# Attention and gated MLP on one core: other blocks for five weight-conversion steps and for the q and k transposes of the next pair

## The chip, the cores and the metric

The kernel runs on one core of a Trainium2 chip. The metric is the device time of one execution in microseconds (us): 690.47, the median of three runs (690.37 to 690.92). Engine names are those of the profile: PE is TensorE (matmuls), PEld its weight loads, DVE is VectorE, ACT is ScalarE, POOL is GpSimd and SP is SyncE, whose queue issues most DMAs.

## The reference

q, k and v have the shape (4 batches, 8 heads, 576 positions, 64). The result of the attention is the input of a gated MLP with three weights.

```python
def rotate(x):
    x1, x2 = (x[..., :half], x[..., half:])
    return np.concatenate([x1 * cos - x2 * sin, x1 * sin + x2 * cos], axis=-1)
scores = 1/np.sqrt(D) * np.matmul(rotate(q), rotate(k).transpose(0, 1, 3, 2))
attn = np.exp(scores - np.max(scores, axis=-1, keepdims=True))
attn = attn / (np.sum(attn, axis=-1, keepdims=True) + 1e-09)
x = np.matmul(attn, v)          # then (batch, position) rows of 8 heads x 64 = 512
g = x @ w_gate                  # 512 x 1536
y = (g / (1 + np.exp(-g))) * (x @ w_val) @ w_out
```

## The kernel before, in words

All matrix work is done in a pair of 32-bit pieces: a value is split into a high part, which a copy to the matmul type makes, and a low part, which a subtraction makes. A product is the sum of high x high, high x low and low x high. So each transpose or product that goes on into another product leaves PSUM twice: ACT casts the high part (for the probabilities L426, for q and k L308, for tails L440), then DVE subtracts it from the source (L427, L312, L441). Only after the subtraction is the PSUM buffer free.

**The attention stage** works on 16 pairs of heads, 9 blocks each: blocks 0 to 7 are 128 rows of one head (head 0 and 1 in turn), block 8 holds the 64 last rows of both. For each of the 144 blocks, numbered n = 9 p + b, TensorE computes scores (L349) into one of two score buffers, DVE takes the row maximum (L364), ACT takes the exponential (L382), TensorE transposes the probabilities in four parts (L425), and ACT and DVE make high and low parts of them. The scores of a block can start only when the exponential of two blocks before has read its buffer. Transposes of any kind share three PSUM buffers. The parts of a row beyond 512 are transposed as tails (L435, L437). When the first four or the last five blocks of a pair are transposed, the products with v follow in 10 matmuls per head (L465) into one buffer, which ACT copies out (L470) and a DMA stores.

**q and k of the next pair** are prepared in this stage. GpSimd rotates them (L206 to L208). In three steps (`qk_T`, L281) TensorE transposes the rotated tile: the tails in 2 transposes (L293), q in 4 and k in 4 (L289); ACT casts each result (L308) and DVE makes the low part (L312). The last of the three steps also issues eight DMAs on SP (`qk_stack`, L314) that copy the finished parts within SBUF into the operands of the scores: QK, QZ and BD.

**The first two weights** are unpacked in the same stage (`wfirst`, L765, with `bits10`, L717): each takes ten steps on ACT (L752, L724, L727), GpSimd (L725, L729 to L731) and DVE (L754 to L756). For every four pairs a row of reciprocals is made (L392, L393), transposed (L400), copied (L402) and stored.

**What sets the order.** A table `PLAN` names, for each step, the block in which the program writes it down. `qk` has three rows, for pair 0, pair 1 and all later pairs: the blocks of the first, second and third step; `qkw` names what each step is (2 is the tails, 0 is q, 1 is k). `cv` has a row for each of the two weights: the block of the load, then the blocks of the ten steps. The loop at L1053 goes through the blocks and through the step functions in the order of L31:

```python
    w, bs = P["qkw"][min(p, 2)], P["qk"][min(p, 2)]
    for i in range(3):
        if bs[i] == b:
            at.qk_T(p + 1, w[i], i == 2)
...
    for i, ns in enumerate(P["cv"]):
        if n == ns[0]:
            cvq[i] = moe.wfirst(0, i)
        for _ in range(ns[1:].count(n)):
            tc.keep_in_program_order(cvq[i].pop(0)())
```

GpSimd keeps the written order throughout; PE keeps it in pair 0 and SP up to block 48. Everything else is put in order by a scheduler at build time, which starts from the written order; so a step that is written elsewhere also moves other instructions. After attention the MLP stages follow, bound to a written order on PE and SP.

Of the kernel before, what the change touches and what calls it, by code (L numbers as in the profile page):

```python
# [28 lines left out]
    trb=3,  # L29
    warm=[9, 0, 1, 2, 0, 1],  # L30
    order=["qk", "scores", "trans", "pv", "exp", "evac", "rstore", "rope", "tails", "conv", "x", "conv1", "vsplit"],  # L31
    qk=[[3, 4, 6], [1, 2, 3], [0, 0, 1]],
    qkw=[[0, 2, 1], [2, 0, 1], [2, 0, 1]],
    tails=[4, 0],
    pv=[1, 6, 5, 3, 7, 8, 2, 7, 3],
# [3 lines left out]
    rope=1,  # L39
    vsplit=8,  # L40
    rstore=0,
    cv=[[13, 21, 25, 26, 28, 30, 34, 34, 44, 44, 45], [20, 30, 35, 36, 39, 41, 43, 43, 54, 54, 63]],
    xs=[[3, 3], [3, 6], [6, 5], [7, 5], [8, 7], [9, 5], [10, 5], [11, 5], [12, 7], [13, 7], [14, 1], [14, 2],
        [14, 8], [15, 0], [15, 2], [15, 4]],
    xe=[[5, 3], [6, 3], [7, 3], [8, 3], [9, 3], [10, 3], [11, 3], [12, 3], [13, 5], [14, 1], [14, 3], [14, 5],
# [1461 lines left out]
```

## Time and profile before

| | |
|---|---|
| time, median of 3 runs | 690.47 us (690.37 to 690.92) |
| the profiled execution | 690.11 us, its span 688.3 us |
| TensorE busy | 677.4 us, 98% of the span |
| VectorE, ScalarE, GpSimd busy | 582.4, 424.2 and 470.1 us |
| attention: scores of block 0 of pair 1 / pair 6 / pair 15 start at | 25.85 / 110.57 / 259.08 us |
| granted TensorE clock | 1.00 throughout |

Times in a timeline are from the start of the span. The busy time of TensorE is modelled: a matmul that overlaps the one before it is shown longer than the engine needs for it, so what an instruction costs is read from the start of one to the start of the next. "<-" behind an instruction names what ended the engine's idle time before it. A merged line such as "x4" stands for neighbours of one kind, at the start of the first.

### The profile page before, as it was taken

Reading aid. Unit: us, or ns where it says so; the run is one execution under the profiler, and the core shown is the slowest. Engines: PE = TensorE matmul, PEld = TensorE weight load, DVE = VectorE, ACT = ScalarE, POOL = GpSimd, SP = SyncE. Lnnn points to the kernel's source line nnn. Section 1 sums busy time; section 2 is a strip of 40 time slices with the busy share of each in tenths; the row PEclk is TensorE's granted clock in tenths of the full one; section 3 lists DMA queues with packets and bytes.
Section 4 is the critical chain, followed back from the end, with each engine's and each line's share of the span. In section 5 each row is a group of like instructions: output and inputs, shape, how many; then the busy total and the mean of one; then the engine's idle time right before and its main releaser. Section 6 shows DMA issues by size and latency. Waiting matters only on the chain. (4 is left out here: it accounts for less than half of the span.)

```text
span 688.3 us, 12675 instructions
## 1 busy us (share of the span) xinstructions
PE 677.4 (98%) x4414; PEld 664.3 (97%) x4414; DVE 582.4 (85%) x883; ACT 424.2 (62%) x873; POOL 470.1 (68%) x475
## 2 busy tenths in 40 slices
PE   7999999999999999999999999999999999999998
PEld 6899999999999999999999999999999999999997
DVE  5888898888888888979988898988999599877683
ACT  5899988888888888555543434424435375344341
POOL 8899799999999985998889588677784720000000
PEclk9999999999999999999999999999999999999999
DMA  6897999889988879791214345354464797627101
GB/s 195 185 248 205 218 225 243 208 206 243 246 206 208 220 189 285 187 235 70 90 58 164 122 141 204 130 187 150 161 212 163 264 317 252 207 74 247 47 24 69
DMA packets 78784, 125.76 MB, mean 183 GB/s; under 512 B 16880, under 2 KB 55680, under 8 KB 78720
## 3 DMA queue, kind: packets, MB, share of 16 engines
q1 hardware_dynamic: 75248, 118.77, 60.6%
q10 hardware_dynamic: 3472, 6.18, 2.4%
q8 instruction: 35, 0.57, 0.4%
q14 instruction: 29, 0.24, 0.1%
HBM read 66.91 MB, written 33.10 MB: 145 GB/s over the span
## 5 line engine op out<-in xcount | busy, mean ns | idle before, releaser
L364 DVE TENSOR_REDUCE nmt<-sc 128x1 f32<-128x576 f32 x144 | 108.2, 751 | 20.3 <-PE sc L349 18.9
L382 ACT ACTIVATE E<-sc,nmt 128x576 f32<-128x576 f32 x128 | 97.5, 761 | 1.7 <-DVE nmt L364 1.6
L425 PE MATMUL tr<-ident,E 128*128 128x128 f32 x512 | 77.1, 274 | 0.4 <-DVE ET1l L427 0.2
L425 PEld LDWEIGHTS tr<-ident,E 128*128 128x128 f32 x512 | 61.2, 141 | 3.4 <-PE tr L289 1.3
L1472 PE MATMUL ch<-dW,dO 128*128 128x384 f32 x216 | 63.8, 337 | 0.2 <-DVE dW L1420 0.2
L206 POOL TENSOR_TENSOR t<-X,tab 128x256 f32<-128x256 f32 (+2 forms) x94 | 54.4, 600 | 9.4 <-DMA X<-in_qk_dram 5.8
L349 PE MATMUL sc<-QK 128*128 128x288 f32 x240 | 58.7, 325 | 1.4 <-ACT E L382 0.6
L426 ACT CAST ET2h<-tr 128x512 fp32r<-128x512 f32 x80 | 47.2, 590 | 14.0 <-PE tr L425 13.7
L427 DVE TENSOR_TENSOR ET2l<-tr,ET2h 128x512 fp32r<-128x512 f32 x80 | 53.1, 682 | 2.1 <-ACT ET2h L426 2.0
L349 PE MATMUL sc<-N,QZ 128*128 128x288 f32 x240 | 51.3, 296 | 0.0
L695 POOL TENSOR_TENSOR W<-WF,W 128x1024 fp32r<-128x1024 f32 x20 | 48.1, 2409 | 3.8 <-ACT W L695 3.7
L208 POOL TENSOR_TENSOR rot<-rot,t 128x512 f32<-128x512 f32 (+2 forms) x47 | 47.0, 999 | 3.7
L427 DVE TENSOR_TENSOR ET1l<-tr,ET1h 128x512 fp32r<-128x512 f32 x64 | 43.0, 685 | 7.0 <-ACT ET1h L426 6.7
L207 POOL TENSOR_TENSOR rot<-X,tab 128x512 f32<-128x512 f32 (+2 forms) x47 | 47.0, 1001 | 0.0
L1472 PE MATMUL ch<-dH,dO 128*128 128x384 f32 x156 | 45.5, 337 | 0.0
L426 ACT CAST ET1h<-tr 128x512 fp32r<-128x512 f32 x64 | 36.9, 597 | 13.1 <-PE tr L425 13.1
L842 PE MATMUL ch<-T2h,W 128*128 128x384 f32 x160 | 44.2, 337 | 0.0
L842 PE MATMUL ch<-T0h,W 128*128 128x384 f32 x160 | 44.2, 337 | 0.0
L842 PE MATMUL ch<-T1h,W 128*128 128x384 f32 x160 | 44.1, 336 | 0.0
L465 PE MATMUL pv<-ET2h,VS 128*128 128x320 f32 x128 | 40.8, 329 | 1.1 <-ACT ET2h L426 0.9
L349 PEld LDWEIGHTS sc<-QK 128*128 128x128 f32 x240 | 36.9, 190 | 4.3 <-ACT E L382 4.1
L1472 PEld LDWEIGHTS ch<-dW,dO 128*128 128x128 f32 x216 | 39.8, 188 | 0.5 <-DVE dW L1420 0.5
(349 smaller groups left out, 2300.7 us busy)
## 6 DMA issues: line engine op xcount, KB each, us to landing
QK<-N SPq DMA_DIRECT2D x64, 288.0 KB, 4.3
hd<-sg SPq DMA_DIRECT2D x14, 768.0 KB, 3.3
dB<-hd SPq DMA_DIRECT2D x8, 1152.0 KB, 7.3
X<-in_qk_dram SPq DMA_DIRECT2D x15, 576.0 KB, 5.6
yd<-Y SPq DMA_DIRECT2D x31, 256.0 KB, 5.7
raw<-in_moe_w_gate_dram SPq DMA_DIRECT2D x12, 512.0 KB, 3.7
raw<-in_moe_w_val_dram SPq DMA_DIRECT2D x12, 512.0 KB, 4.0
Xab<-yd SPq DMA_DIRECT2D x32, 192.0 KB, 4.9
```

Of the source, the lines that this page charges most:

```text
L206: e.tensor_tensor(out=sel(t2, u), in0=sel(x, w), in1=tb(Sn, u), op=ALU.mult)
L207: e.tensor_tensor(out=o, in0=x, in1=tb(C, slice(0, D)), op=ALU.mult)
L208: e.tensor_tensor(out=o, in0=o, in1=t2, op=ALU.add)
L349: nc.tensor.matmul(ps[:, g, 0:288], l, rr[:, o + g * 288:o + (g + 1) * 288], start=(x == 0), stop=(x == len(terms) - 1))
L364: nc.vector.tensor_reduce(out=nmcol, in_=ps[:, :, 0:288], axis=AX.XY, op=ALU.max, negate=True)
L382: nc.scalar.activation(out=E.rearrange("p (a b) -> p a b", a=2), in_=ps[:, :, 0:288], func=ACTF.Exp, bias=nmcol, scale=1.0, accum_out=self ...
L425: nc.tensor.transpose(ps[:, c], E[:, o + c * 128:o + (c + 1) * 128], self.ident)
L426: nc.scalar.copy(dst[0], src)
L427: nc.vector.tensor_tensor(out=dst[1], in0=src, in1=r32(dst[0]), op=ALU.subtract)
L695: return [lambda: self.nc.scalar.copy(h, f), lambda: le.tensor_tensor(out=l, in0=f, in1=r32(h), op=ALU.subtract)]
L842: nc.tensor.matmul(acc, l[:, w, c * 128:(c + 1) * 128], r, start=(n == 0 and k not in ONTO), stop=(n == 5), skip_group_check=True)
L1472: nc.tensor.matmul(ps, l, r[:, f], start=(new and f == 0 and x == 0), stop=(f == NFP - 1 and x == 2), skip_group_check=True)
```

## The change

Only the table changes. In pair 1 the three q and k steps of the next pair are written in blocks 0, 1 and 2 in place of 1, 2 and 3; from pair 2 on in blocks 0, 1 and 2 in place of 0, 0 and 1. Of the conversion, three steps of the first weight go from blocks 30, 34 and 34 to 29, 30 and 31, and two of the second from 35 and 36 to 33 and 34.

```diff
-    qk=[[3, 4, 6], [1, 2, 3], [0, 0, 1]],
+    qk=[[3, 4, 6], [0, 1, 2], [0, 1, 2]],
...
-    cv=[[13, 21, 25, 26, 28, 30, 34, 34, 44, 44, 45], [20, 30, 35, 36, 39, 41, 43, 43, 54, 54, 63]],
+    cv=[[13, 21, 25, 26, 28, 29, 30, 31, 44, 44, 45], [20, 30, 33, 34, 39, 41, 43, 43, 54, 54, 63]],
```

TensorE in an even pair (pair 9), before, from the scores of block 1 to the transposes behind those of block 3. L349 is scores, L289 q or k, L425 with Et the probabilities of block 8, L435 and L437 tails, L465 the products with v:

```order
L349 MATMUL sc<-QK_112 128x288 x2
L349 MATMUL sc<-N_111,QZ_114 128x288 x2
L289 MATMUL tr<-ident,rot 128x128 x4
L425 MATMUL tr<-ident,Et 128x128 x4
L349 MATMUL sc<-QK_112 128x288 x2
L349 MATMUL sc<-N_111,QZ_114 128x288 x2
L435 MATMUL tr<-ident,E 128x128 x2
L437 MATMUL tr<-ident,Et 128x2x64
L349 MATMUL sc<-QK_112 128x288 x2
L349 MATMUL sc<-N_111,QZ_114 128x288 x2
L289 MATMUL tr<-ident,rot 128x128 x4
L465 MATMUL pv<-ET2h,VS_115 128x320
```

The same place in the changed program:

```order
L349 MATMUL sc<-QK_112 128x288 x2
L349 MATMUL sc<-N_111,QZ_114 128x288 x2
L425 MATMUL tr<-ident,Et 128x128 x4
L349 MATMUL sc<-QK_112 128x288 x2
L349 MATMUL sc<-N_111,QZ_114 128x288 x2
L435 MATMUL tr<-ident,E 128x128 x2
L437 MATMUL tr<-ident,Et 128x2x64
L465 MATMUL pv<-ET2h,VS_115 128x320
L289 MATMUL tr<-ident,rot 128x128 x4
L349 MATMUL sc<-QK_112 128x288 x2
L349 MATMUL sc<-N_111,QZ_114 128x288 x2
L425 MATMUL tr<-ident,E 128x128 x4
```

q's four transposes went from behind the scores of block 1 to behind the tails, and the first matmul of the products with v went ahead of them; k's transposes, which stood last before, now come behind the scores of block 4.

ScalarE in the same place, before, from the exponential of block 0 (first row) to that of block 3 (last row); L470 copies the products out, L308 casts q and k, L426 probabilities, L440 tails:

```order
L382 ACTIVATE E,sumt<-sc,nmt 128x576
L470 COPY Y_2460<-pv 128x256
L308 CAST N_91<-tr 128x512
L382 ACTIVATE E,sumt<-sc,nmt 128x576
L426 CAST ET2h<-tr 128x4x2x64
L440 CAST TK2h<-tr 128x384
L382 ACTIVATE E,sumt<-sc,nmt 128x576
L308 CAST N_91<-tr 128x512
L426 CAST ET1h<-tr 128x4x128
L382 ACTIVATE E,sumt<-sc,nmt 128x576
```

And in the changed program:

```order
L382 ACTIVATE E,sumt<-sc,nmt 128x576
L470 COPY Y_2460<-pv 128x256
L308 CAST N_91<-tr 128x3x64
L426 CAST ET2h<-tr 128x4x2x64
L382 ACTIVATE E,sumt<-sc,nmt 128x576
L440 CAST TK2h<-tr 128x384
L382 ACTIVATE E,sumt<-sc,nmt 128x576
L308 CAST N_91<-tr 128x512
L426 CAST ET1h<-tr 128x4x128
L382 ACTIVATE E,sumt<-sc,nmt 128x576
```

The cast ahead of block 1's exponential was q's; now the tails' small cast (3x64) and that of block 8's probabilities stand there, and q's comes two exponentials later.

ScalarE at the start of pair 4, before, from the exponential of pair 3's block 8 to that of block 2; L727 and L724 are conversion steps of the first and the second weight, L402 copies the transposed reciprocals:

```order
L382 ACTIVATE Et,sumt<-sc,nmt 128x576
L426 CAST ET2h<-tr 128x4x128
L308 CAST N_111<-tr 128x3x64
L385 COPY Et<-Et 128x64
L727 CAST FO<-raw 128x512
L382 ACTIVATE E,sumt<-sc,nmt 128x576
L470 COPY Y_1167<-pv 128x256
L724 ACTIVATE raw<-raw 128x512
L308 CAST N_111<-tr 128x512
L426 CAST ET2h<-tr 128x4x2x64
L382 ACTIVATE E,sumt<-sc,nmt 128x576
L402 COPY rr<-tr 36x128
```

And in the changed program, to the exponential of block 2:

```order
L382 ACTIVATE Et,sumt<-sc,nmt 128x576
L426 CAST ET2h<-tr 128x4x128
L382 ACTIVATE E,sumt<-sc,nmt 128x576
L385 COPY Et<-Et 128x64
L470 COPY Y_1168<-pv 128x256
L308 CAST N_111<-tr 128x3x64
L426 CAST ET2h<-tr 128x4x2x64
L402 COPY rr<-tr 36x128
L382 ACTIVATE E,sumt<-sc,nmt 128x576
L440 CAST TK2h<-tr 128x384
L382 ACTIVATE E,sumt<-sc,nmt 128x576
```

Both conversion steps and q's cast left the place, and the copy of the reciprocals now stands ahead of block 1's exponential instead of behind it.

## Rows read from the trace of the kernel before

**Rows 1.** The page, part 1: busy time of each engine.

```profile
PE 677.4 (98%) x4414; PEld 664.3 (97%) x4414; DVE 582.4 (85%) x883; ACT 424.2 (62%) x873; POOL 470.1 (68%) x475
```

**Rows 2.** Windows, pairs 1 to 5 and 6 to 14: length, then busy.

```profile
core 0: us, PE busy (x) PEld busy (x) DVE busy (x) ACT busy (x) POOL busy (x), PEclk, DMA share, GB/s
25.85:110.57 84.72, 82.56 (x642) 79.09 (x641) 74.60 (x123) 75.48 (x191) 75.69 (x85) 1.00 0.89 219
110.57:259.08 148.51, 147.59 (x1167) 143.64 (x1165) 130.33 (x212) 131.61 (x335) 139.44 (x163) 1.00 0.87 220
```

**Rows 3.** The list of waits: us in total, times, longest.

```profile
PEld sc L349 <- ACT E L382: 4.1, 12, 0.6
```

**Rows 4.** Timeline of pair 9, blocks 1 to 3: start, length, engine, instruction.

```profile
162.59 0.43 PE L349 MATMUL sc<-QK 128*128 128x288 f32 x2
...
163.12 0.60 PE L289 MATMUL tr<-ident,rot 128*128 128x128 f32 x4
...
163.32 0.76 DVE L364 TENSOR_REDUCE nmt<-sc 128x1 f32<-128x576 f32 x1
...
163.56 0.60 PE L425 MATMUL tr<-ident,Et 128*128 128x128 f32 x4
163.76 0.59 ACT L308 CAST N<-tr 128x512 fp32r<-128x512 f32 x1 [0.19 <-PE tr L289]
...
164.24 0.75 ACT L382 ACTIVATE E<-sc,nmt 128x576 f32<-128x576 f32 x1
...
164.75 0.27 PE L437 MATMUL tr<-ident,Et 128*128 128x128 f32 x1
...
165.13 0.30 PEld L349 LDWEIGHTS sc<-QK 128*128 128x128 f32 x2 [0.34 <-ACT E L382]
...
166.11 0.39 PE L465 MATMUL pv<-ET2h,VS 128*128 128x320 f32 x1
...
166.48 0.63 PE L425 MATMUL tr<-ident,E 128*128 128x128 f32 x4
```

**Rows 5.** Timeline of pair 4, blocks 0 to 2.

```profile
78.33 0.69 ACT L727 CAST FO<-raw 128x512 fp32r<-128x512 f32 x1
...
79.80 0.53 PE L349 MATMUL sc<-QK 128*128 128x288 f32 x2
79.86 0.71 ACT L724 ACTIVATE raw<-raw 128x512 f32<-128x512 uint32 x1
...
81.58 0.41 PE L465 MATMUL pv<-ET2h,VS 128*128 128x320 f32 x1 [0.88 <-ACT ET2h L426]
...
82.09 0.30 ACT L402 COPY rr<-tr 36x128 f32<-36x128 f32 x1
...
82.41 0.51 PE L349 MATMUL sc<-QK 128*128 128x288 f32 x2
```

**Rows 6.** Timeline of pair 5, blocks 0 and 1.

```profile
95.91 0.50 PE L349 MATMUL sc<-QK 128*128 128x288 f32 x2
96.01 0.69 ACT L727 CAST FO<-raw 128x512 fp32r<-128x512 f32 x1
...
97.48 0.52 PE L349 MATMUL sc<-QK 128*128 128x288 f32 x2 [0.22 <-ACT E L382]
```

**Rows 7.** Pair 9's copies: k's subtraction, SP's issues, pair 10's first scores, landing of L323.

```profile
167.38 0.68 DVE L312 TENSOR_TENSOR N<-tr,N 128x512 fp32r<-128x512 f32 x1
...
169.84 0.61 SPq L319 DMA_DIRECT2D QK<-N  x1
...
172.48 1.07 SPq L323 DMA_DIRECT2D QK<-N  x1
...
176.59 0.51 PE L349 MATMUL sc<-QK 128*128 128x288 f32 x2
...
DMA to landing us min/median/max: 3.9/4.6/7.1
```

**Rows 8.** Timeline: one conversion step (L754) of each weight, and GpSimd.

```profile
67.94 0.41 DVE L754 TENSOR_SCALAR raw<-raw 128x512 uint32<-128x512 uint32 x1
...
88.62 1.29 POOL L208 TENSOR_TENSOR rot<-rot,t 128x512 f32<-128x512 f32 x1
...
88.99 1.20 DVE L754 TENSOR_SCALAR raw<-raw 128x512 uint32<-128x512 uint32 x1
```

## The prediction, written before the changed kernel ran

> **What bounds the kernel now.** The page comes first: TensorE is busy for 98% of the span and no other engine comes near it [rows 1]. So only time in which TensorE stands still, or in which it is held between two matmuls, can be won. The change touches the attention stage alone, so the stretches come next, cut at the first score matmul of pairs 1, 6 and 15 [rows 2]: pairs 1 to 5 take 84.72 us, or 16.94 each, and pairs 6 to 14 take 148.51, or 16.50 each. The reader is to see that TensorE is nearly full in both, that ScalarE and VectorE are each at 88%, and that GpSimd is at 94% in the second. Nothing here is far from full, so an order that frees one engine easily runs into the next. The granted clock is 1.00 in both rows, so no part of the sum comes from it. The list of waits then names what TensorE's weight loads wait for: first of all ScalarE's exponential, which has to read a score buffer before the next scores go into it [rows 3]. There are two such buffers, so the scores of one block wait for the exponential of two blocks before.
>
> The timeline of pair 9, a pair of the even stretch, shows this loop [rows 4]. Scores of block 1 start at 162.59, their reduction at 163.32, their exponential at 164.24, and the scores of block 3, which need the freed buffer, at 165.13: 2.54 us in all. The exponential started 1.65 after the scores because ScalarE was casting q's transposes (163.76) just ahead of it. TensorE's own work in the loop, by the starts in the same rows: four score matmuls 0.53 (162.59 to 163.12), four transposes 0.44 (163.12 to 163.56), twice each, and three tail transposes at 0.11, 0.33: 2.27. Against 2.54 it stood for about 0.3, and the row says so itself: 0.34 until E. A second hold follows: from 166.11 to 166.48 one matmul of 320 columns takes 0.37, where one of 288 takes 0.53 / 4 = 0.13 and so one of 320 about 0.15. That is 0.22. Together some 0.5 us per pair.
>
> **The q and k steps.** No instruction is added or taken away; 10 transposes, 3 casts, 3 subtractions and 8 copies by DMA per pair are placed elsewhere. In pairs 2 to 14 q's step goes from block 0 to 1 and k's, with the copies, from 1 to 2; in pair 1 all three go a block sooner. By the order of the changed program the scores of blocks 1 and 3 now stand 0.53 + 0.44 (transposes of block 8) + 0.53 + 0.33 + 0.15 (one value matmul) + 0.44 (q) = 2.42 us of TensorE work apart instead of 2.27. The loop's other side is unchanged: the transposes that follow the scores still start 0.53 after them, their cast 0.64 later as at 163.76, the exponential 0.48 after that, the next scores 0.89 later: 2.54. The wait falls from 0.34 to 0.12. The second hold should go, since the transposes behind that value matmul now follow a score wait that gives their buffer time to be freed. At best a pair gains 0.34 + 0.22 - 0.12 = 0.44. Against it: on ScalarE the copy of the value output and the tail cast now both stand ahead of the cast of block 8 and so of that exponential. If they keep it late by 0.25, the gain is 0.19. I take 0.30, nearer the middle, since nothing decides. For nine pairs, 6 to 14: **2.7 us** (1.7 to 4.0; if the wait grows to 0.6, a loss of 0.4). In pairs 8 and 12 the small copy of the row sums (L402) now stands ahead of block 1's exponential, and its transpose comes only after the scores of block 2; I take 0.2 back for each: **-0.4**.
>
> The cover is the freed slack in blocks 4 to 8. There the new order puts two transposes of E side by side with a block of tails between them. Before already runs that order once, from the end of pair 4 into pair 5: its scores at 95.91 came without a wait, and the next, at 97.48, waited only because the conversion cast at 96.01 (0.69 us) stood ahead of their exponential [rows 6]. In the pairs after it no conversion is there.
>
> **The conversion steps.** The table moves five entries: the second VectorE step of the gate weight by one block (29 for 30), its cast to block 30 and the VectorE step behind it to 31 (from 34), and ScalarE's scaling and GpSimd's clamp of the value weight by two. In pair 4 before, the cast (78.33, 0.69) and the scaling (79.86, 0.71) stand on ScalarE among the exponentials, and TensorE pays [rows 5]: scores at 79.80, the next at 82.41, 2.61 us, of which the work is 0.53 + 0.11 + 0.15 + 0.33 = 1.12. So 1.5 are lost, 0.88 of them in one row. With both gone the row-sum copy still holds the exponential: its transpose follows the scores of block 2 by 0.53, a cast follows its last transpose by about 0.3 (0.64 less three starts of 0.11), the copy takes 0.30, and the next scores follow the exponential by 0.89: 2.0, with q's 0.44 now inside. That saves 0.6, and 0.44 of work moves in that was done elsewhere: 1.0. I take **0.7** (0.3 to 1.5), since the subtractions around it are not walked through. The same steps now weigh on pair 3, where 0.69 of ScalarE and 0.36 of VectorE come in; ahead of them blocks without q's cast give room. Pairs 1 to 5 lie 5 x 0.44 = 2.2 above the even ones; less pair 4's 0.7 that leaves 1.5 to be won in pairs 1, 2, 3 and 5 at best, and at worst pair 3 pays the cast. I take **0.3** (-0.7 to 1.5). The GpSimd clamp goes ahead of the value split of pair 4; what waits for that split is the load of the next values, used a pair later: nothing.
>
> One price is open: how long a conversion step takes on VectorE. The same operation took 0.41 us at 67.94 and 1.20 at 88.99, where GpSimd had been in a rotation since 88.62 [rows 8]. The Trainium skill (SBUF — State Buffer, Who interferes with whom) speaks against such a move: VectorE and GpSimd share a port pair under an exclusive lock, and a VectorE scalar operation in a two-port mode waits for the whole GpSimd instruction. The row agrees, with 1.20 for 0.41. By that rule a moved step may land behind a rotation and cost 0.8 more, and the sum would be 0.8 smaller. By the rows alone it stays as it is, since GpSimd is as full where the steps stood.
>
> **Sum:** 2.7 - 0.4 + 0.7 + 0.3 = 3.3. What follows attention is TensorE-bound and its order is unchanged, so it starts that much sooner. The profiled execution took 690.11 us (span 688.3, the rest lies around it), 0.36 under the median of the three runs, 690.47. The forecast is 690.5 - 3.3 = **687.2 us**. A measurement here can tell about 0.2%, 1.4 us, from no change.
>
> **Rivals.** *The wait only moves (same).* ScalarE is at 88%, and its queue from block 8 to block 1 holds casts, copies and exponentials without a break; then the exponential of block 1 is late by as much as was won, 0.0 to 0.1 per pair, and pair 4's 0.7 less 0.4 is left, with at most 0.6 from the rest: 689.8. For it: ScalarE's share. Against it: 2.42 of work against 2.27 in the same loop.
>
> *The copies come late (slower).* The score operands of the next pair are copied within SBUF after k's subtraction. In pair 9 that subtraction starts at 167.38, the last big copy is issued at 172.48 and lands 4.6 later (median; up to 7.1), at 177.1, while the next pair starts at 176.59 and needs this copy one block on, some 2.4 later, at 179.0: 1.9 to spare [rows 7]. k's step is now a block, about 1.5, later. It decides when issue slips by more than 1.9, or when the landing is nearer 7.1. Late by 0.4 in each of the 13 pairs it costs 5.2, and 5.2 - 3.3 = 1.9 slower: 692.4. Against it: before, the copies waited behind others in SP's queue for 1.8 us after the subtraction, and in the new order those others stand ahead and are done by then.
>
> *GpSimd becomes the bound (between).* It is busy 139.44 us in pairs 6 to 14, 15.5 per pair [rows 2]; a pair of 16.2 still covers that, so this ends the gain only past 0.9 per pair. I give it no chance of its own. That the change does nothing is excluded for q and k by the order; the five entries do move rows.
>
> **Chances.** Forecast 0.62, the wait only moves 0.28, the copies come late 0.10. So faster by over 0.2% 0.62, within 0.2% 0.28, slower 0.10. **Range:** the terms at their best, 4.0 - 0.4 + 1.5 + 1.5 = 6.6, lie together only rarely; I set the low end at 6.0 below: 684.5. The high end takes in the wait that only moves (689.8) and a part of the late copies: 691.2.
>
> **What would show it.** Pairs 6 to 14 should take about 16.2 us each (146 for the stretch of 148.51), and the wait of weight loads for E should shrink in the list. In pair 4 the gap of 2.61 should be near 2.0. If ScalarE's row ahead of block 1's exponential shows no idle and the wait for E stands at 0.3 or more, the first rival is right. If a score matmul waits for a DMA into QK or QZ at the start of a pair, the second is. A changed length of anything behind attention would be wrong by every case here.

## The result and the profile after

The changed kernel took **700.05 us** (median of 4 runs, 699.57 to 701.08), the kernel before on the same chip 690.66 (690.37 to 690.92): a ratio of **1.0139**, 95% interval 1.0124 to 1.0154. The profiled execution has a span of 699.3 us against 688.3, so 11.0 us are to be found; it is the slowest of the four, and the medians differ by 9.4. The forecast was 687.2.

TensorE did the same work; its share fell because the span grew (the page, part 1, as [rows 1]):

```profile
PE 679.5 (97%) x4414; PEld 666.1 (95%) x4414; DVE 583.4 (83%) x883; ACT 425.8 (61%) x873; POOL 469.8 (67%) x475
```

The windows view of the changed kernel, with the columns of [rows 2], cut at the first score matmul of pairs 1, 6, 8, 10, 14 and 15:

```profile
26.12:110.22 84.10, 81.98 (x642) 79.15 (x641) 74.66 (x122) 75.43 (x191) 76.68 (x86) 1.00 0.87 225
110.22:142.64 32.42, 32.42 (x261) 31.93 (x260) 28.42 (x47) 29.36 (x75) 31.14 (x37) 1.00 0.88 219
142.64:177.47 34.83, 32.84 (x263) 31.98 (x261) 31.16 (x50) 30.80 (x78) 33.22 (x40) 1.00 0.88 219
177.47:243.05 65.58, 65.34 (x517) 63.91 (x518) 57.01 (x93) 58.44 (x149) 61.17 (x73) 1.00 0.81 210
243.05:263.39 20.34, 16.44 (x129) 15.98 (x130) 15.10 (x25) 16.03 (x40) 7.07 (x8) 1.00 0.83 214
```

The reader is to see that the change did what was meant, and where it was undone. Pairs 1 to 5 take 84.10 us for 84.72. Pairs 6 and 7 take 16.21 each; before, pairs 6 to 14 took 16.50 on average [rows 2]. Pairs 8 and 9 together take 34.83, about 1.8 more than two average pairs before. Pair 14 alone takes 20.34, and its TensorE is busy for only 16.44 of that.

The wait that the change was to shorten did shrink: 4.1 us in 12 waits before [rows 3], and in the changed kernel's list of waits:

```profile
PEld sc L349 <- ACT E L382: 1.3, 2, 0.9
```

In TensorE's timeline the hole is one row:

```profile
263.39 0.56 PE L349 MATMUL sc<-QK 128*128 128x288 f32 x2 [3.90 <-DMA QK<-N]
```

The scores of pair 15 wait 3.90 us for the copies of q and k. The windows of that hole, and of block 0 of pair 15 right behind it, show a second price, in the granted clock (the last but two of the columns):

```profile
259.50:263.39 3.89, 0.00 (x0) 0.03 (x1) 0.83 (x2) 1.32 (x3) 0.00 (x0) 1.00 1.06 241
263.39:267.18 3.79, 3.79 (x18) 3.78 (x19) 2.05 (x3) 1.46 (x4) 0.53 (x1) 0.55 1.04 304
```

TensorE stood still, and for the next 3.79 us its granted clock was 0.55: mostly the lower of its two levels (1.2 of 2.4 GHz). Before, that block took 2.24 us (from the row at 259.08 to the scores of block 1 at 261.32), so the low clock cost 1.55.

Why the copies were late is seen in SP's issues. The timeline of SP, first before, then after, with "..." where rows are left out (L319 to L323 copy q and k of pair 15; L772 and L780 load 512 KB of MLP weights each; L630 reads row sums for the MLP's x):

```profile
250.32 0.61 SPq L319 DMA_DIRECT2D QK<-N  x1
...
252.63 1.34 SPq L323 DMA_DIRECT2D QK<-N  x1
...
257.04 1.23 SPq L630 DMA_DIRECT2D R<-rd  x2
...
260.90 0.57 SPq L772 DMA_DIRECT2D raw<-in_moe_w_gate_dram  x1
261.51 0.48 SPq L772 DMA_DIRECT2D raw<-in_moe_w_val_dram  x1
262.80 1.54 SPq L780 DMA_DIRECT2D raw<-in_moe_w_gate_dram  x2
```

```profile
251.49 0.35 SPq L772 DMA_DIRECT2D raw<-in_moe_w_gate_dram  x1
251.89 1.07 SPq L772 DMA_DIRECT2D raw<-in_moe_w_val_dram  x1
253.05 0.62 SPq L319 DMA_DIRECT2D QK<-N  x1
...
255.65 1.43 SPq L323 DMA_DIRECT2D QK<-N  x1
...
264.40 1.37 SPq L780 DMA_DIRECT2D raw<-in_moe_w_gate_dram  x2
...
268.76 0.58 SPq L630 DMA_DIRECT2D R<-rd  x1
```

The copies are issued 2.7 us later, since k's step is a block later and the issue of the loads stands ahead. The two weight loads, 1 MB, are issued 9.4 us sooner, and so go ahead of the copies. The time from issue to landing of that first copy (L319), before and after:

```profile
DMA to landing us min/median/max: 4.1/4.1/4.1
```

```profile
DMA to landing us min/median/max: 8.9/8.9/8.9
```

Behind attention the loss grows on. The first MLP product (L794) starts at 281.77 for 276.06, 5.7 late; by the end it is 11.0. Of the 5.3 between the two, all but 0.4 is lost by 352 us, at a granted clock of 1.00. TensorE's timeline there has four waits of 0.25 us or more, and none before the change. Three are at this product; the fourth, 1.12 us at 346.92, is for VectorE (L817):

```profile
305.20 0.62 PE L794 MATMUL ch<-xa,w1h 128*128 128x384 f32 x2 [0.27 <-DVE Xab L809]
309.91 0.61 PE L794 MATMUL ch<-xm,w1h 128*128 128x384 f32 x2 [0.27 <-DVE Xab L809]
318.41 0.62 PE L794 MATMUL ch<-xm,w0h 128*128 128x384 f32 x2 [1.70 <-ACT sv L808]
```

Together they are 3.36 of the 5.3; the rest is in smaller gaps. The list of waits names GpSimd, which prepares the MLP's x from the loads of L637. First before, then after (us in total, times, longest):

```profile
POOL Xab L644 <- DMA Xab<-yd: 8.2, 3, 3.7
```

```profile
POOL Xab L644 <- DMA Xab<-yd: 18.9, 3, 12.6
```

It stood 12.6 us for one x load, issued at 257.17 behind the weight loads and copies above and 8.6 us on its way. What it prepares then comes late; that the four waits hang on this is argued, not shown.

### The profile page after: what moved, and what is told of

Read it like the earlier page. It is cut to its first block, busy times and chain, and to the rows that moved or that the text cites. A ratio compares the mean times of both kernels' runs of the same rounds, so it can differ in the third digit from the quotient of the medians.

```text
span 699.3 us, 12732 instructions
## 1 busy us (share of the span) xinstructions
PE 679.5 (97%) x4414; PEld 666.1 (95%) x4414; DVE 583.4 (83%) x883; ACT 425.8 (61%) x873; POOL 469.8 (67%) x475
## 2 busy tenths in 40 slices
DMA packets 78784, 125.76 MB, mean 180 GB/s; under 512 B 16880, under 2 KB 55680, under 8 KB 78720
## 5 line engine op out<-in xcount | busy, mean ns | idle before, releaser
L425 PE MATMUL tr<-ident,E 128*128 128x128 f32 x512 | 77.8, 274 | 0.0
L349 PE MATMUL sc<-QK 128*128 128x288 f32 x240 | 59.1, 327 | 6.4 <-DMA QK<-N 4.7
L425 PEld LDWEIGHTS tr<-ident,E 128*128 128x128 f32 x512 | 61.4, 141 | 1.9 <-issue 0.7
L206 POOL TENSOR_TENSOR t<-X,tab 128x256 f32<-128x256 f32 (+2 forms) x94 | 54.0, 596 | 5.4 <-DMA X<-in_qk_dram 1.5
L426 ACT CAST ET2h<-tr 128x512 fp32r<-128x512 f32 x80 | 47.0, 588 | 13.6 <-PE tr L425 12.9
L349 PE MATMUL sc<-N,QZ 128*128 128x288 f32 x240 | 51.7, 297 | 0.0
L349 PEld LDWEIGHTS sc<-QK 128*128 128x128 f32 x240 | 36.9, 190 | 8.8 <-issue 4.5
L465 PE MATMUL pv<-ET2h,VS 128*128 128x320 f32 x128 | 41.1, 331 | 0.1
L426 ACT CAST ET1h<-tr 128x512 fp32r<-128x512 f32 x64 | 37.5, 611 | 3.3 <-PE tr L425 3.2
```

The lines of the kernel that those rows point to most:

```text
L206: e.tensor_tensor(out=sel(t2, u), in0=sel(x, w), in1=tb(Sn, u), op=ALU.mult)
L349: nc.tensor.matmul(ps[:, g, 0:288], l, rr[:, o + g * 288:o + (g + 1) * 288], start=(x == 0), stop=(x == len(terms) - 1))
L425: nc.tensor.transpose(ps[:, c], E[:, o + c * 128:o + (c + 1) * 128], self.ident)
L426: nc.scalar.copy(dst[0], src)
```

## The experiments

**Theory A:** small copies that stand behind big loads land late, and each such wait, with the lower clock behind it, makes up the loss. **Rival C:** k's step in block 2 is by itself too late. **Rival D:** what is lost behind attention has a cause of its own.

### Which half of the change

Run qk_only is the kernel before with the new rows of q and k, cv_only with the new conversion blocks. The edit of qk_only:

```diff
-    qk=[[3, 4, 6], [1, 2, 3], [0, 0, 1]],
+    qk=[[3, 4, 6], [0, 1, 2], [0, 1, 2]],
```

> Only the q and k rows of the table are changed; the conversion steps stay where they were before. In its SP queue the two weight loads of 512 KB each stand ahead of pair 14's four big QK copies, as in the changed kernel. Theory A (the loss is queue order: copies that the next pair needs stand behind big loads): nearly the whole loss of 9.4 us is here, 697 to 701 us. Rival B (the conversion steps cost it): 687 to 690 us.

> Only the conversion steps are moved. SP's queue in pair 14 is as before: the QK copies stand ahead of the weight loads. Theory A: within 1.5 us of the kernel before, 689 to 692 us. Rival B: 697 us or more.

qk_only took 696.44 us, ratio 1.0086 (1.007 to 1.0103), a little under theory A's 697 to 701; cv_only 690.69, 1.0001 (0.9991 to 1.001). The conversion blocks alone do nothing to the time. Beside the new rows they matter: pair 4 takes 17.52 us before, 16.89 in cv_only, 19.14 in qk_only and 16.60 with both. The q and k rows alone put the line 772 loads ahead of the copies, and TensorE waits 2.35 us ahead of pair 15. But in qk_only nothing was lost behind attention: 6.4 us late at the first MLP product, 5.7 at the end. There the last x loads went out before that product; in the changed kernel they went out after it.

### SP's queue in written order

Run spone126 is the changed kernel with SP's instructions kept in the order in which they are written from pair 14 on; in spone_all they are kept so through all of attention. TensorE's order in attention is the changed kernel's. The main part of spone126's edit:

```diff
-        if n == 48:
-            ctl0.__exit__(None, None, None)
+        if n in (48, 126):
+            ctl0 = sp_order(tc, ctl0, n == 48)
...
```

> The changed kernel, with SP's queue held in the written order from pair 14 on: the QK copies of pair 14 now stand ahead of the weight loads; TensorE's order in the attention stage is the same. Theory A: the wait of 4.1 us ahead of pair 15 goes, and with it most of what follows it: 690 to 694 us, and the scores of pair 15 start at about 259 us. Rival C (k's step a block later is too late by itself, whatever stands ahead in the queue): a wait of 2 us or more stays ahead of pair 15, 697 us or more. Rival D (the losses after attention have their own cause): the wait goes, but some 5 us stay behind the end of attention, 695 us.

> The changed kernel, with SP's queue in the written order throughout attention. Theory A: as the kernel with the order held from pair 14, and also without the wait of 1.1 us ahead of pair 10, which stands behind the row-sum loads: 688 to 692 us. Rival C: waits at the start of most pairs, since now every copy is issued in one block behind k's subtraction: 700 us or more.

They took 700.35 us, 1.014 (1.0123 to 1.0157), and 704.56, 1.0192 (1.0164 to 1.0221); both miss theory A's times. In spone126 the wait ahead of pair 15 is gone with k's step where it was and the last copy (L323) issued at 255.73, as late as in the changed kernel: pair 14 takes 16.22 and pair 15 starts at 259.20. That excludes rival C for this wait. The gain is given back at once, because the line 772 loads now go out at 270.39. VectorE's timeline there:

```profile
277.28 1.05 DVE L751 TENSOR_SCALAR raw<-raw 128x512 uint32<-128x512 uint32 x1 [6.84 <-DMA raw<-in_moe_w_gate_dram]
278.25 0.68 DVE L427 TENSOR_TENSOR ET1l<-tr,ET1h 128x512 fp32r<-128x512 f32 x1
```

A weight conversion stands in VectorE's order and waits for its load; the attention subtraction queued behind it waits too, and TensorE stands 6.13 us for that one. spone_all has the same stall (6.49), and the wait ahead of pair 10, which was to go, is 2.07 there: for that pair the written order is no remedy.

### Pair 15's copies first, or on another queue

Run old14 uses before's row in pair 14 alone (tails and q in block 0, k in block 1), which puts the four copies ahead of the loads; mid_011 has k's step one block sooner in all pairs from 2 on, which does so too; act15 leaves all written steps and issues pair 15's copies from ScalarE; pin_raw holds the line 772 loads behind the row-sum reads, and the scheduler puts the line 780 loads in their place.

```diff
-    qk=[[3, 4, 6], [0, 1, 2], [0, 1, 2]],
+    qk=[[3, 4, 6], [0, 1, 2], [0, 1, 2], [0, 0, 1]],
...
-        w, bs = P["qkw"][min(p, 2)], P["qk"][min(p, 2)]
+        w, bs = P["qkw"][min(p, 2)], P["qk"][3 if p in (14,) else min(p, 2)]
```

> The changed kernel, but in pair 14 alone the step for pair 15 uses the row of before (q in block 0, k's two in blocks 0 and 1). SP's order there becomes: the four QK copies of pair 15, two Xab loads, then the two 512 KB weight loads; the rows for the MLP keep the changed kernel's order more nearly than before's. Theory A (the loss ahead of pair 15 is the queue: 1 MB of loads ahead of the copies): the wait of 4.1 us in pair 14's block 8 and the 1.5 us of pair 15's block 0 go, pair 14 back to 16.4, first score matmul of pair 15 at about 259.2 instead of 263.4, and the time 700.0 - 5 = 695 if the MLP's stalls stay, 690 if they go too. Rival C (k's step in block 2 is by itself too late): the same for this pair, so this run does not tell A from C. Rival D (the stalls behind attention have their own cause, late R and Xab loads): these stay where the R and Xab loads of the last pairs come after the weight loads, some 5 us.

```diff
-    qk=[[3, 4, 6], [0, 1, 2], [0, 1, 2]],
+    qk=[[3, 4, 6], [0, 1, 2], [0, 1, 1]],
```

> The changed kernel with k's second step one block sooner in pairs 2 to 14: row [0, 1, 1] for [0, 1, 2]. SP's order at the end of the stage becomes: four QK copies, two Xab loads, first weight load. Theory A and rival C: no wait ahead of pairs 10 and 15, the time at or under 690.7; if the even pairs keep the 0.25 us that the changed kernel won (16.2 instead of 16.46) then 688.0, if two steps in one block cost it again 690. Rival D: Xab and R loads are late as in the changed kernel and some 5 us of stalls stay behind attention, 693 to 695.

```diff
-        d = self.nc.sync.dma_start
+        d = (self.nc.scalar if p == 15 else self.nc.sync).dma_start
```

> The changed kernel, but pair 15's eight copies inside the chip go out on ScalarE's queue instead of SP's; k's last step stays in block 2 and the two weight loads go out when they did. Theory A in its queue form (the copies stand behind 1 MB in the same queue): copies land 3 to 5 us after issue instead of 8.9, and the wait of 4.1 us ahead of pair 15 goes. Theory A in its bandwidth form (the DMA engines are shared, whatever the queue): the copies still need 8 us or so from issue, and most of the 4.1 us stays. Rival C (k's step is too late by itself): the 4.1 us stays whatever the queue. Time 695 to 696 by the queue form, 700 by the others.

```diff
-        self.nc.sync.dma_start(out=tmp[:, 0:1024], in_=self.wsrc(i, f))
+        d = self.nc.sync.dma_start(out=tmp[:, 0:1024], in_=self.wsrc(i, f))
+        if f:
+            self.tc.keep_in_program_order(d)
```

> The changed kernel with the two weight loads of line 772 (1 MB in all) held behind the R and Xab loads; the scheduler then puts the two loads of line 780 (also 512 KB each) in their place ahead of pair 15's copies. PE's order is the changed kernel's. Theory A: any 1 MB ahead does it, so the wait of about 4 us ahead of pair 15 stays, and the time stays 700 or grows, since the held loads now feed DVE late. If the wait were special to the loads of line 772 (what reads them, where they land), it would go: 695.

old14 took 697.42 us, 1.0108 (1.0063 to 1.0153); mid_011 697.59, 1.0098 (1.0068 to 1.0128); act15 702.55, 1.0169 (1.0144 to 1.0194); pin_raw 704.55, 1.0229 (1.0173 to 1.0285). old14 and mid_011 miss theory A's times (690 to 695, and 690.7 or less).

In old14 pair 15 starts at 258.81, sooner than before, and a stall comes up further on. ScalarE's row, TensorE's, and the window behind:

```profile
277.22 0.37 ACT L470 COPY Y<-pv 128x256 f32<-128x256 f32 x1 [3.69 <-DMA yd<-Y]
```

```profile
277.64 0.39 PE L465 MATMUL pv<-ET1h,VS 128*128 128x256 f32 x1 [3.38 <-ACT Y L470]
```

```profile
277.60:283.00 5.40, 5.36 (x26) 5.36 (x27) 3.21 (x5) 3.61 (x9) 5.07 (x6) 0.68 0.84 217
```

ScalarE may not overwrite Y until its store has landed, and that store, issued at 267.20 behind the line 780 loads, took 9.9 us. It reads as the same mechanism with another victim (the next section moves those loads), and the clock fell again, to 0.68. mid_011 has the same row (TensorE 3.62 at 281.69), and in its pair 2 copies came late as well (1.18 and 1.55). In pin_raw the wait ahead of pair 15 is 2.10, with other loads in front, so nothing is special to line 772; the held loads then stop VectorE as in spone126 (6.42).

act15 tells two forms of theory A apart. ScalarE's issues, and the landing of the first of them:

```profile
251.93 0.63 ACTq L319 DMA_DIRECT2D QK<-N  x1
252.66 1.18 ACTq L320 DMA_DIRECT2D QK<-N  x1
253.88 1.15 ACTq L322 DMA_DIRECT2D QK<-N  x1
256.03 0.49 ACTq L323 DMA_DIRECT2D QK<-N  x1
256.56 0.58 ACT L426 CAST ET1h<-tr 128x512 fp32r<-128x512 f32 x1 [3.62 <-DMA raw<-in_moe_w_gate_dram]
```

```profile
DMA to landing us min/median/max: 8.0/8.0/8.0
```

On their own queue the copies still take 8.0 us, the later ones 10.6 and 11.6 (by then a third load was under way). So their place in SP's queue is not the cause: copies and loads share what carries them. The Trainium skill (DMA: Bandwidth & Descriptors, Issuing engines are not separate DMA queues) says so: DMAs from different engines end up on the same 16 DMA engines and interleave. This run agrees. Those engines are full around here in both kernels; the windows of 255 to 265 us, before and after, with the DMA share last but one:

```profile
255.00:265.00 10.00, 10.00 (x82) 9.82 (x81) 8.56 (x15) 8.93 (x25) 5.99 (x7) 1.00 1.02 250
```

```profile
255.00:265.00 10.00, 6.10 (x47) 5.88 (x45) 4.83 (x8) 5.23 (x13) 0.00 (x0) 0.94 1.01 243
```

The page gives 125.76 MB moved in each kernel; the order decides who is late. ScalarE's issues cost something as well: it came to its next cast only at 256.56, after 3.62 us without work, and TensorE stood 2.65 at 258.02 for what hung on it. The scheduler also put TensorE's work from 250 us on, in pair 14, in another order and sent a line 780 load ahead, at 252.25. So this run speaks of the landing alone: pair 15 starts at 264.44, and the only wait for its copies over 0.3 us is 0.48, a block later.

### The line 780 loads

The back_ runs write the two line 780 loads behind the x reads that follow them; the ia_ runs issue them right behind pair 14's first store of Y.

```diff
-    S.load()
-    S.load()
     moe.rload(1, 1, None, 2)
     moe.rload(1, 1, None, 3)
     moe.yload(1, 1)
+    S.load()
+    S.load()
```

> The kernel before with the same two loads of line 780 moved back: the control. In the kernel before nothing on TensorE waits there, so theory A says no change, 690.7 within 0.7. If it gets slower, the later loads cost something of their own (their first use is at about 288 us, some 12 us after they would go out); if faster, the kernel before lost time there too.

> The run old14 (pair 15's copies issued ahead of the line 772 loads), with the two 512 KB loads of line 780 written behind the row-sum and x reads that feed the MLP's first products, so that they no longer stand ahead of pair 14's store of Y. Theory A in its bandwidth form (what is small lands late when big loads are under way with it): the 3.4 us stall of the old14 run at 273.7 us, where ScalarE's copy into Y waits for the store of Y's last contents, goes, and with it the 1.4 us at the lower granted clock behind it; the time falls by about 5 from 697.4, to 690 to 693, and the rest over before is pairs 8 and 9 (1.1 and 0.7). Rival D (the MLP's start is late for a reason of its own, not the loads): the stall stays, 696 to 698.

> As back_old14, and pair 9's step for pair 10 also in before's blocks (the row [0, 0, 1]), so that pair 10's copies go out one block sooner. Theory A: the 0.7 to 1.3 us wait at the end of pair 9 goes as well and the time is 0.5 to 1 under that of back_old14, 689 to 692, which is before's time give or take 1; a version under before's 690.7 would need pair 8's 1.0 us back too. If the waits at pair 9's end were another cause's (pair 8's late sums, which this run leaves), nothing changes against back_old14.

> The changed kernel with the two loads of line 780 alone moved back as in back_old14; the two of line 772 stay ahead of pair 15's copies. Theory A: the wait of 3.9 to 4.7 us ahead of pair 15 and the lower clock behind it stay (about 5.7 of drift at the first MLP product), and the stalls of the next 70 us (another 4.8 of drift: late Xab and row-sum reads) shrink, since those reads no longer stand behind 1 MB more: 700.0 falls to 695 to 698. If those stalls are GpSimd's own (it is simply late since attention is), they stay: 700.

These missed by too large a step: the loads went out between 294 and 300 us and were themselves late. back_before, the control, took 697.72 us, 1.0099 (1.0084 to 1.0114), and TensorE's timeline in it shows why:

```profile
301.19 0.61 PE L794 MATMUL ch<-xa,w0h 128*128 128x384 f32 x2 [2.96 <-ACT Xab L808]
```

The others took 700.63 us, 1.0141 (1.0126 to 1.0157), 700.14, 1.0133 (1.0118 to 1.0148), and 703.48, 1.0182 (1.0156 to 1.0207), and do not tell the theories apart in the total. One thing in back_old14 does: its first MLP product starts at 276.40, against 279.44 in old14 and 276.06 before, and the stall behind the store of Y is 1.20 us there (at 267.75) for 3.38, once those loads are not ahead of it.

```diff
-    S.load()
-    S.load()
+    with moe.tc.issue_after(y0):
+        S.load()
+        S.load()
...
```

> The kernel before with the line 780 loads behind the same store: the control for the move by itself. Theory A: the loads have some 15 us of slack there, so no change, 690 to 691.5. If the move costs by itself, that shows here (the back_before run lost 6.8 with the loads 30 us later).

> The run old14 (pair 15's copies ahead of the line 772 loads), with the two 512 KB loads of line 780 issued right behind pair 14's first store of Y (267 us) instead of ahead of it; they then go out near 268 to 273 us, well ahead of their first use near 288 us. Theory A: neither the wait ahead of pair 15 (gone in old14) nor the 3.4 us stall at 273.7 us with 1.4 us of lower clock behind it is left, and the loads are not late as in the back_ runs: 690 to 692, over before by what pairs 8 and 9 lose less what the even pairs gain. Rival D: the MLP's start still stalls some 5 us, 696 to 698.

> The changed kernel with the line 780 loads behind pair 14's store of Y; the line 772 loads stay ahead of pair 15's copies. Theory A: the wait of 4 us ahead of pair 15 and the lower clock behind it stay, drift at the first MLP product about 5.7; what is lost behind it (4.8 more in the changed kernel) shrinks, if the loads were what held back the row-sum and x reads: 695 to 698. Rival: those losses only follow from the late end of attention or from GpSimd: 700.

> As ia_old14, and the row sums' store one block later (pairs 4, 8 and 12), so that its transpose no longer stands in the queue of TensorE ahead of the sums it waits for (0.86 + 0.59 in pair 8). If pair 8's extra 1.0 us is that wait: pair 8 back to 16.2 to 16.5, time 0.5 to 1.5 under ia_old14; if the wait only moves, the same time.

ia_before: 691.4 us, 1.0005 (0.9996 to 1.0014), so the small move is free. ia_old14: 696.63, 1.0074 (1.0051 to 1.0098). Neither the wait ahead of pair 15 nor the stall of 3.38 behind Y is there, and attention ends without a large hole. It missed the 690 to 692 expected: pair 15 starts 2.5 us late (pair 9 takes 17.93, 1.5 over before), and 5.3 more is lost behind the first MLP product, as much as in the changed kernel. ia_after: 703.75, 1.0179 (1.0162 to 1.0196), a miss: its pair 15 waits 2.96, and further on ScalarE stands 5.66 for an x load behind the moved loads, TensorE 4.66 behind it. ia_old14_rs1 (the row sums' step one block later): 698.89, 1.0117 (1.0062 to 1.0171). Its pair 8 takes 17.59 against 17.58: that wait only moves.

### The MLP's start, and the gains alone

Run fix_old14 is ia_old14 with the line 772 loads behind the row-sum reads. Run early3_7 is the kernel before with the new conversion blocks and the new row in pairs 3 to 7 only; SP's order at the end is then before's.

```diff
-                cv1[i] = moe.wfirst(1, i)
+                with tc.issue_after(moe.lastr.ins):
+                    cv1[i] = moe.wfirst(1, i)
...
```

> ia_old14, and the line 772 loads held behind the two row-sum reads that the MLP's first x groups need, as they stand in the kernel before. In ia_old14 TensorE still lost some 4 us between 285 and 345 us, where GpSimd had waited for those reads (issued at 264, landed at 272 to 274; in the kernel before issued at 257). Theory A: the reads land 3 to 5 us sooner and those losses shrink to 2 or less, 693 to 695 for ia_old14's 696.6. Theory A's own price: the second of the held loads goes out at about 267 and VectorE may wait for it in its order as in the run spone126 (6.3 us there). If the losses at 285 to 345 stay while the reads land sooner, they have another cause.

```diff
-    qk=[[3, 4, 6], [0, 1, 2], [0, 1, 2]],
+    qk=[[3, 4, 6], [1, 2, 3], [0, 0, 1], [0, 1, 2]],
...
-        w, bs = P["qkw"][min(p, 2)], P["qk"][min(p, 2)]
+        w, bs = P["qkw"][min(p, 2)], P["qk"][3 if p in range(3, 8) else min(p, 2)]
```

> The kernel before with the new conversion blocks, and the new row [0, 1, 2] in pairs 3 to 7 alone; all other pairs keep before's rows. SP's order from pair 11 on is then before's, with the copies of pair 15 ahead of the loads. Theory A: the gains of the changed kernel where no copy is late: pair 4 about 0.9, pairs 6 and 7 0.25 each, pair 5 0.15 lost, pair 8 within 0.5 either way where the rows change back; pair 15 starts some 1 us sooner than 259.08 and nothing behind it is lost: 689.3 to 690.3, ratio 0.998 to 0.9995. Rival (the gains are taken back by any late wait, or each shift of the stage upsets the queue at its end): 690.7 or more.

fix_old14 took 695.51 us, 1.0055 (1.0038 to 1.0073). The reads land at 267.5 and 270.4 for 272.3 and 273.9, yet the wait at the product of the changed kernel's row at 318.41 stays, 1.77 for 1.71, so the reads are not its cause. They are not without effect: behind the first MLP product 2.9 us are lost, for 5.3 in ia_old14, though that product starts 1.2 later. What goes with the wait at that product is the last x load. That load goes out before the first MLP product in before (by 4.8 us), early3_7 (4.8), ia_before (3.8), spone126 (2.2) and qk_only (1.6), and none of these waits at that product. It goes out after it in the changed kernel (2.7), ia_old14 (3.4), fix_old14 (1.9), old14 (2.5) and ia_after (4.1), and these wait 1.70, 1.71, 1.77, 0.60 and 0.78; cv_only and spone_all (4.7 and 1.6 before, no wait) and act15, ia_old14_rs1, back_old14 and back_old9_14 (2.7 to 3.5 after, waits of 0.55 to 1.71) fit too. mid_011 and back_after, 1.0 and 3.8 after, do not wait there; pin_raw and back_before, 3.3 and 3.7 before, wait 0.45 and 0.55. So the cause looks again like a late small transfer, of x, and rival D is the less likely, not excluded. This is a pattern with four exceptions, not a test: no run moved those x loads alone.

early3_7 took 692.6 us (12 runs, 690.21 to 694.26), 1.0023 (1.001 to 1.0036), for 689.3 to 690.3 by theory A. Pair 15 starts 3.74 us late, the first MLP product 3.60, the span ends 3.4 late: with SP's order of before nothing is lost at the end, as theory A has it. But the gains did not reach the total. SP's timeline ahead of pair 6, and TensorE's row:

```profile
98.59 4.18 SPq L175 DMA_DIRECT2D X<-in_qk_dram  x2
102.98 0.62 SPq L319 DMA_DIRECT2D QK<-N  x1
103.69 0.61 SPq L320 DMA_DIRECT2D QK<-N  x1
```

```profile
112.55 0.50 PE L349 MATMUL sc<-QK 128*128 128x288 f32 x2 [1.68 <-DMA QK<-N]
```

Two loads of 576 KB now stand ahead of pair 6's copies. The copy of L322 takes 7.6 us to land there, for 4.6 before. Behind this shorter hole, too, the granted clock was low, 0.58 over the next 3.50 us, and pair 6 took 17.96 us for 16.46. The 1.38 that pair 3 lost is not traced. No version tried beats the kernel before.

## Why the prediction was wrong

- **Even pairs, +2.7: the mechanism held, in four pairs of nine.** The wait for E shrank as said. Pairs 6, 7, 10 and 11 are 0.24 to 0.29 shorter for the 0.30 forecast; pairs 12 and 13 won nothing (16.72 and 16.47), and 8, 9 and 14 lost.
- **Pair 4, +0.7: right.** Its gap of 2.61 [rows 5] became 1.98, where 2.0 was worked out, and the pair is 0.92 shorter. Pairs 1 to 5 gained 0.62 together for the 1.0 forecast; in it pair 2 lost 1.65 and pair 3 won 1.23. Part of pair 2's loss is late copies again: its second block waits 0.55 for QK (at 45.85), whose last copy landed after 7.5 us for 4.8 before.
- **Pairs 8 and 12, -0.4: too small for pair 8.** It lost 0.88: the transpose of the row sums waits 0.70 for VectorE's reciprocal, and a tail transpose 0.45 behind it. Pair 12 lost 0.08.
- **The open price of a conversion step beside GpSimd: right to be left out.** L754 took 0.41 and 1.20 before [rows 8], 0.68 and 1.04 after. GpSimd was in a rotation beside the 0.41 as well (L206, which began at 67.94 too), so these rows are not one step alone and one beside it.
- **The step that failed** is the dismissal of "the copies come late": "in the new order those others stand ahead and are done by then". What stands ahead in SP's order at the end of the stage was never looked at. It was 1 MB of weights for the MLP, and landing took 8.9 us and more, where the rival reckoned with 4.6 to 7.1 [rows 7], the median and the longest of the copies of L323 that the trace times. The 7.1 was the copy issued at 252.63, pair 15's own: the slowest landing was at this place already before. The copies slipped by 2.7 (L319) to 3.0 us (L323), where 1.5 was reckoned and 1.9 was to spare. The rival priced the last copy; pair 15 waited for the first two, which landed at 262.0 and 263.3. That rival also spread the cost evenly, 0.4 in each of 13 pairs; it came at pair 14 (3.88) and, it seems, pair 9 (0.83), where other loads lie. The trace puts pair 9's wait down to ScalarE here, and to these copies in act15, back_after and pin_raw.
- **"What follows attention ... starts that much sooner" failed too.** Its TensorE order is unchanged, but its data come by the same queue. After pair 15's start the loss grew by 1.55 at the low clock and by 5.3 behind the first MLP product. The closing test, that a changed length of anything behind attention would be wrong by every case, came true.
- **A slip that changed nothing:** the first rival's 689.8 does not follow from its terms; 690.5 less 0.3 and at most 0.6 is 689.6.

Of the 11.0 us, then: 4.3 net by the start of pair 15 (3.9 of it the wait that spone126 and old14 take away, with 0.27 lost ahead of pair 1 and the other gains and losses nearly even), 1.4 more by the first MLP product, 5.3 behind it. The first two are shown; the cause of the 5.3 is not. This is the split of one execution: pair 9 took 17.30 us here, 16.89 in pin_raw and 16.47 in ia_after, with the same order on TensorE. What stays open besides is whether an order exists that keeps the gains with nothing late, and how the 5.3 would split if the x loads alone were moved.

## What to carry to other kernels

A step that moves on the compute engines moves its transfers too, and where a scheduler orders a queue it may let the loads of the next stage pass them. So read the DMA queue's new order up to the end of the stage, not in one typical round, and price a small copy by what is under way with it: here 4.1 us with no weight load ahead of it and 8 to 12 us beside 1 MB or more. Where the DMA engines are full, moving one transfer can make another late, as in old14, spone126 and ia_after; look for the waits of stores that free a buffer and of in-order conversions, not only of the operand at hand.

## What had not been expected of the hardware

- Copies within SBUF issued from another engine landed no sooner: 8.0 to 11.6 us from ScalarE's queue, 8.9 to 9.9 from SP's, with 1 MB of loads under way in both (1.5 MB behind ScalarE's later ones).
- A hole in TensorE is dearer than its length: behind the 3.90 us of the changed kernel the granted clock was 0.55 over the next 3.79 us (1.55 lost), behind the 1.68 us of early3_7 0.58 over 3.50 us, and 0.68 over 5.4 us behind the 3.38 us hole of old14, where twelve products took 3.60 us from start to start of what follows (279.44 to 283.04) for 2.17 before (276.06 to 278.23).
- Executions of one kernel differ: early3_7 ranged over 4 us, the kernel before over 2.5 beside it. One execution of each was profiled, so what makes the difference is not shown; early3_7's waits for copies are a candidate.
